# The output layer of a fused attention and feed-forward kernel: from two chunks at a time inside the gated streams to a stage of its own with seven products

## The chip, the cores and the metric

The kernel runs on one core of a Trainium2 chip. TensorE multiplies into PSUM; VectorE (DVE in the profile), ScalarE (ACT) and GpSimd (POOL) work on SBUF; SyncE (SP) issues the DMA transfers between SBUF and device memory. The metric is the device time of one execution in microseconds (us): the median of several runs. A profile comes from one further execution on the same core.

## The reference

Attention with a sigmoid, a feed-forward layer with a maximum of three products, and a gated feed-forward layer, one after the other:

```python
scores = scale * np.matmul(q, k.transpose(0, 1, 3, 2)) - np.log(S)     # q, k, v: 4 x 12 x 448 x 64
attn = np.matmul(1.0 / (1.0 + np.exp(-scores)), v)
x = np.ascontiguousarray(attn.transpose(0, 2, 1, 3)).reshape(B * S, H * D)       # 1792 x 768
h = np.maximum(np.maximum(x @ w1, x @ w2), x @ w3)                     # 768 x 768 each
x = h @ w_out                                                          # 768 x 768
g = x @ w_gate                                                         # 768 x 1536
silu = g * (1.0 / (1.0 + np.exp(-g)))
val = x @ w_val                                                        # 768 x 1536
return silu * val @ w_out2                                             # 1536 x 768; 1792 x 768 comes out
```

The change is about the last product, `silu * val @ w_out2`, and about how the products before it are summed. The weights come as 64-bit floats and are turned into 32-bit ones on the chip.

## The kernel before

Every matrix product is done with split operands: each 32-bit factor is a high part (a cast by ACT or DVE, L351) and a low part (the subtraction of the high part from the factor, on DVE or POOL, L354), and three of the four products of parts are added (`PRODUCTS`). So one product over 128 contraction rows is three matmul instructions, all of them from line L922.

The 1792 rows are worked in two parts: s=0 holds rows 0 to 767, s=1 rows 768 to 1791. A part is two blocks of n columns, n=384 for s=0 and n=512 for s=1. After attention come the first layer, the second layer, then `gated(1)` and `gated(0)`.

Four of the layers' products go through `stream` (L1051): a 768-wide factor is cut in halves both ways, and instead of eight block products seven products of sums of halves are made (A11·B11, S2·T2, A12·B21, S3·T3, A22·T4, S1·T1, S4·B22), nine matmuls each. Each product gets a PSUM bank of its own (`m` and `av` in turn), and DVE adds the bank to a running sum in SBUF (`plus`, L1078). The left factors of a stream (tiles `w`, a ring of five) come from DRAM in `gated(0)`: `gated(1)` stored them split (`ds_S`, `ds_A`), and `seven` loads them (L572) into the tiles (A11, A12), (S2, S3), (A22), (S1, S4). The right factors (tiles `T00` to `T26`) stay for all twelve streams of a part; for s=0 `recall` loads the rows kept in DRAM and makes them, with one instruction per 384 columns.

`gated(s)` runs six times over: a gate stream (whose four results go through Silu on ACT), a value stream (whose results are multiplied with those, L1148, and split into tiles `g`), and, one round late, `last(i)`: with the 256 rows of w_out2 that belong to i (tile `wr`, from `rows_pair`), each of the part's 128-row chunks (8 for s=1, 6 for s=0) gets two outputs of 384 columns, six matmuls each. The first round copies the two banks (tile `mm`) into an SBUF tile `o`; the next ones add to it (L1206, 768 wide); the final round adds 384 columns at a time (L1216) and sends them to `out` (L1223). The final `last` of `gated(1)` stands between the streams of `gated(1)` and those of `gated(0)`, and while it runs, `recall` is worked on DVE, ACT and POOL.

What sets the order: every step is a task with costs per engine and a due time, and a planner (`Plan.order`) lists them; each engine then works its list strictly in order, and waits at an instruction whose inputs are not there. The products keep program order on TensorE. SP too issues its DMAs in the listed order, each one when its tile is free.

## Time and profile before

| | |
|---|---|
| median of three runs | 975.11 us (974.92 to 975.33) |
| span of the profiled execution | 976.3 us |
| TensorE matmul busy | 961.4 us, 98% of the span, 5099 instruction records |
| VectorE busy | 646.9 us, 66% |
| ScalarE busy | 429.0 us, 44% |
| GpSimd busy | 147.2 us, 15% |
| DMA | 214 GB/s on the mean |
| `gated(1)` | about 498 to 766 us |
| `gated(0)` | about 766 to 976 us |

The profiled execution has no time other than its span, from the first to the last instruction; the span is 1.2 us over the median. Sums are made against the span, and 1.2 us is taken off at the end. "Busy" is a share of the whole span; which engine ends a wait differs from stage to stage, so the views of a stretch count for more than these shares. TensorE instructions overlap: the pitch from one group's start to the next one's start is what a group costs, and it is shorter than the busy time shown for it. The same holds for DVE.

### The profile page before, as it was taken

The numbers are of one execution on the slowest core, as the hardware profiler recorded it, in microseconds if no ns is written. First come the engines' busy times: TensorE is split into PE (matmuls) and PEld (weight loads), VectorE is DVE, ScalarE is ACT, GpSimd is POOL, SyncE is SP. The second block draws the span as 40 slices with busy tenths as digits, with TensorE's granted clock in tenths as the row PEclk, the third lists the DMA queues.
The fourth block names the chain that finished last, engine by engine and source line by source line (L and its number), as shares of the span: only waits on it lengthen the run. The fifth ranks groups of instructions, "written<-read, shape, count | busy, mean of one in ns | idle before, by whom it ended". The sixth has DMA issues, their size and how long they took to land.

```text
span 976.3 us, 13569 instructions
## 1 busy us (share of the span) xinstructions
PE 961.4 (98%) x5099; PEld 814.7 (83%) x5099; DVE 646.9 (66%) x971; ACT 429.0 (44%) x603; POOL 147.2 (15%) x117
## 2 busy tenths in 40 slices
PE   9989999999999999999999999999999999999998
PEld 4435677767999888888878989888898999999998
DVE  5565667676777888964588396958587743455545
ACT  5666576686666555513355461615253322111110
POOL 0100000000110132210012031425334300000000
PEclk9999999999999999999999999999999999999999
DMA  6677899997998755433357474847588865557532
GB/s 123 119 142 176 241 241 273 243 274 247 313 318 302 230 189 178 140 127 138 113 192 271 168 288 155 298 162 276 198 306 304 299 234 195 193 194 254 187 139 100
DMA packets 179297, 208.51 MB, mean 214 GB/s; under 512 B 98080, under 2 KB 154656, under 8 KB 179232
## 3 DMA queue, kind: packets, MB, share of 16 engines
q1 hardware_dynamic: 177376, 207.42, 66.6%
q8 instruction: 40, 0.66, 0.3%
q10 hardware_dynamic: 1856, 0.23, 0.2%
q14 instruction: 25, 0.20, 0.1%
HBM read 132.91 MB, written 74.71 MB: 213 GB/s over the span
## 4 chain that ended last, share of the span: by engine, by line
PE 81%; DMA 8%; DVE 4%; SPq 4%; issue 1%; ACT 1%; DVEq 0%; ACTq 0%
PE m L922 32%; PE av L922 25%; PE mm L922 18%; SPq L708 3%; PE av L805 3%; PE ps L776 2%; DMA wraw<-in_moe_w_out_dram 2%; DMA rk<-in_k_dram 1%; DMA dp<-c 1%; DMA rq<-in_q_dram 1%; DMA wraw<-in_moe_w_gate_dram 1%; DMA rv<-in_v_dram 1%; DMA wraw<-in_moe_w_val_dram 1%; DVE kT L746 0%; PE ps L769 0%
## 5 line engine op out<-in xcount | busy, mean ns | idle before, releaser
L922 PE MATMUL av<-T,w 128*128 128x512 f32 (+1 forms) x1044 | 235.8, 369 | 0.7 <-DVE T L354 0.7
L922 PE MATMUL m<-T,w 128*128 128x512 f32 (+1 forms) x1035 | 233.1, 369 | 0.0
L922 PEld LDWEIGHTS av<-T,w 128*128 128x128 f32 x1044 | 191.0, 188 | 26.7 <-DVE T L354 1.1
L922 PEld LDWEIGHTS m<-T,w 128*128 128x128 f32 x1035 | 189.5, 188 | 25.7
L922 PE MATMUL mm<-wr,g 128*128 128x384 f32 x840 | 147.7, 334 | 0.1
L922 PEld LDWEIGHTS mm<-wr,g 128*128 128x128 f32 x840 | 145.9, 188 | 0.9 <-DVE o L1206 0.4
L922 PEld LDWEIGHTS m<-x,w 128*128 128x128 f32 x648 | 112.4, 189 | 12.6 <-issue 8.1
L922 PE MATMUL m<-x,w 128*128 128x384 f32 x648 | 120.0, 340 | 0.0
L1078 DVE TENSOR_TENSOR u<-m,u 128x512 f32<-128x512 f32 (+1 forms) x75 | 48.1, 645 | 75.1 <-PE m L922 74.7
L789 ACT ACTIVATE a<-ps,bias 128x896 f32<-128x896 f32 x84 | 80.7, 1003 | 30.2 <-PE ps L776 25.8
L1206 DVE TENSOR_TENSOR o<-mm,o 128x768 f32<-128x768 f32 x56 | 53.4, 955 | 47.2 <-PE mm L922 47.2
L805 PE MATMUL av<-a,rv 128*64 128x448 f32 (+1 forms) x384 | 76.4, 562 | 2.0 <-DVE x L354 1.6
L776 PEld LDWEIGHTS ps<-qq,kk 64*128 64x128 f32 x432 | 45.4, 252 | 34.1 <-ACT a L789 23.9
L776 PE MATMUL ps<-qq,kk 64*128 64x448 f32 x432 | 61.0, 406 | 6.9 <-ACT a L789 6.7
L450 ACT ACTIVATE r<-wraw 128x768 int32<-128x768 uint32 x48 | 43.7, 911 | 50.9 <-DMA wraw<-in_moe_w_gate_dram 14.4
L354 POOL TENSOR_TENSOR g<-t,g 128x512 fp32r<-128x512 f32 (+1 forms) x21 | 28.3, 1348 | 249.7 <-ACT g L351 240.6
L471 DVE SCALAR_TENSOR_TENSOR c<-c,r 128x768 int32<-128x768 int32 x48 | 49.2, 1025 | 18.6 <-ACT r L463 17.9
L1078 DVE TENSOR_TENSOR u<-av,u 128x512 f32<-128x512 f32 (+1 forms) x72 | 45.9, 641 | 20.7 <-PE av L922 20.4
L351 ACT COPY u<-av 128x512 f32<-128x512 f32 (+1 forms) x17 | 9.3, 549 | 112.4 <-PE av L922 112.4
L805 PEld LDWEIGHTS av<-a,rv 128*64 128x64 f32 (+1 forms) x384 | 20.1, 136 | 39.0 <-issue 29.4
L463 ACT ACTIVATE r<-wraw 128x768 f16<-128x768 f32 x48 | 52.2, 1087 | 0.6
L351 ACT CAST g<-t 128x384 fp32r<-128x384 f32 (+1 forms) x43 | 23.9, 560 | 56.9 <-DVE t L1148 52.2
(109 smaller groups left out, 1104.8 us busy)
## 6 DMA issues: line engine op xcount, KB each, us to landing
ds_S<-w SPq DMA_DIRECT2D x24, 768.0 KB, 4.5
w<-ds_S SPq DMA_DIRECT2D x24, 768.0 KB, 5.1
dp<-c SPq DMA_DIRECT2D x42, 384.0 KB, 4.9
cc<-dp SPq DMA_DIRECT2D x21, 768.0 KB, 4.9
wraw<-in_moe_w_dram SPq DMA_DIRECT2D x18, 768.0 KB, 5.9
wraw<-in_moe_w_gate_dram SPq DMA_DIRECT2D x12, 768.0 KB, 5.8
wraw<-in_moe_w_val_dram SPq DMA_DIRECT2D x12, 768.0 KB, 5.1
ds_A<-w SPq DMA_DIRECT2D x12, 768.0 KB, 5.4
```

Source lines behind the costliest of these rows:

```text
L351: (eng.copy if eng is nc.scalar else eng.tensor_copy)(o, i)
L354: eng.tensor_tensor(out=o, in0=a, in1=b, op=ALU.subtract)
L450: lambda e: e.activation(rb_at(), word(0).bitcast(U32), AF.Copy, scale=0.875 * 2.0 ** -29, bias=0.4999),
L463: lambda e: e.activation(rb_at().bitcast(F16).rearrange("p (c two) -> p c two", two=2)[:, :, 1], word(1).bitcast(F32), AF.Copy, scale=2.0 ...
L471: lambda e: e.scalar_tensor_tensor(c_at().bitcast(I32), c_at().bitcast(I32), 3, rb_at(), ALU.logical_shift_left, ALU.bitwise_or),
L708: eng.dma_start(out=r.t[D * j + 32 * e:D * j + 32 * e + 32], in_=src[b, h0 + j, :, 32 * e:32 * e + 32].rearrange("(c i) d -> i c d", i=32),)
L776: nc.tensor.matmul(psb.t[:, j, :S], kk.t[half_p[j], wh, cols], qq.t[half_p[j], xh], start=(i == 0), stop=(i == 2),)
L789: lambda e: e.activation(ab.t, psb.t[:, :, :S], AF.Sigmoid, bias=bias, scale=SCALE),
L805: nc.tensor.matmul(accs[g].t[half_p[j], :S], pairs[g][2].t[at, j, c], ab.t[at, j], start=first[g], stop=last[g],)
L922: nc.tensor.matmul(acc.at(n), l(), r(), start=(i == 0), stop=(i == len(terms) - 1))
L1078: lambda e: e.tensor_tensor(out=o.t[:, :n], in0=acc.at(n), in1=x.t[:, :n], op=ALU.add),
L1206: lambda e, o=o, b=banks[0].b: e.tensor_tensor(out=o.t, in0=b.t[:, :, :NO], in1=o.t, op=ALU.add),
```

## The change

`last` and `rows_pair` go. The products of gate and value are no longer split there: those of s=0 stay in SBUF (tile `G0`), those of s=1 go to DRAM (24 stores of 256 KB), and a new stage `output` at the very end multiplies them with w_out2, again as seven products of sums of halves: the contraction (1536) and the 768 output columns are cut in halves, and so are the rows, where one chunk takes 128 rows of block 0 and 128 of block 1 of the same part. There are seven chunks (three of s=0, four of s=1), seven products each, 18 matmuls of 128x384 a product: 882, where `last` had 1008. The weights w_out2 are turned into 32-bit numbers during streams 2 to 9 of `gated(0)` and four streams of `gated(1)` (`rows_ahead`; 768 KB in, 384 KB out to DRAM each), and loaded again for the new stage (tile `W`, four loads). Sums and splits of both factors are made in the stage, on DVE, ACT and POOL.

In `stream` the products are reordered, and two products that are added go to the same bank: A12·B21 onto A11·B11, S3·T3 and A22·T4 onto S2·T2, S4·B22 onto S1·T1. Before a product is added to a bank, the earlier sum in the bank must have been read. A22·T4 is done late, behind A11·B11 of the next stream. The left tiles are loaded in the order (A11, A12), (S2, S3), (S1, S4), (A22). `recall` makes its sums with instructions of 3x384 columns. The evictions of attention get a due time (`FREE`).

```diff
-    LEFT = (("A11", "A12"), ("S2", "S3"), ("A22",), ("S1", "S4"))
+    LEFT = (("A11", "A12"), ("S2", "S3"), ("S1", "S4"), ("A22",))
...
-    RIGHT = ("B11", "T2", "B21", "T3", "T4", "T1", "B22")
+    RIGHT = ("B11", "T2", "T1", "B21", "T3", "B22", "T4")
...
     def stream(s, left, facs, use, into=None, gated_=True):
...
-        p1 = mult("A11", "B11")
+        mult("A11", "B11", one, True, False)
+        catch_up()
+        u0, w0 = plain(one)
+        mult("S2", "T2", two_, True, False)
+        u1 = half.buf("u", [P, 512])
+        w1 = plus(u1, two_, u0, "u")
+        mult("S1", "T1", three, True, False)
+        v5, w5 = plain(three)
+        mult("A12", "B21", one, False, True, w0)
...
+            use(0, 0, one)
...
+        mult("S3", "T3", two_, False, False, w1)
+        w2 = done(1, 1, two_, v5)
+        mult("S4", "B22", three, False, True, w5)
+        done(0, 1, three, u1)
+
+        def rest_():
+            mult("A22", "T4", two_, False, True, w2)
+            done(1, 0, two_, u0)
+
+        behind.append(rest_)
...
+    OUTER = ("A11", "A12", "S2", "S3", "A22", "S1", "S4")
...
+        def evict(o, acc, x, key=None):
+            plan.add(
+                {"dve": t_dve(NO)},
+                lambda e: e.tensor_tensor(out=o.t[:, :NO], in0=acc.at(NO), in1=x.t[:, :NO], op=ALU.add),
...
+        fetch_g(0)
+        fetch_w(2)
+        fetch_g(1)
+        for q in (1, 3, 0):
+            fetch_w(q)
+        for q in (2, 3):
+            fetch_g(q)
+        for x, name in enumerate(OUTER):
             plan.kind = "w"
...
+            wf = weights(x)
+            for s, c in chunks:
+                k = s, c
+                plan.kind = "w"
+                if name == "A12":
+                    sums(A, k, 2, 2, 3, ALU.add, (), True)
+                if name == "S2":
+                    sums(A, k, 0, 2, 0, ALU.subtract, read[s, c, "A11"])
+                if name == "S3":
+                    sums(A, k, 0, 3, 0, ALU.subtract, read[s, c, "S2"] + s4[k])
+                wb, hl = factor(s, c, name)
+                if name == "S2":
+                    s4[k] = sums(A, k, 1, 1, 0, ALU.subtract, read[s, c, "A12"], True)
```

Three places show the order. In the lists L922 of before is L926 of after, L1078 is L1160, L354 is L358, and L1148 is L1272.

**A stream of `gated(0)`, TensorE.** In the names, T01 is the right factor of the first third of the contraction for the product with index 1, `w_...` is the left tile, `m`, `av` and `mm` are banks. Before, from A11·B11 on:

```order
L922 MATMUL m_8647<-T00_6954,w_8474 128x384 x3
L922 MATMUL m_8647<-T10_6975,w_8474 128x384 x3
L922 MATMUL m_8647<-T20_7232,w_8474 128x384 x3
L922 MATMUL av_8663<-T01_6980,w_8599 128x384 x3
L922 MATMUL av_8663<-T11_7173,w_8599 128x384 x3
L922 MATMUL av_8663<-T21_7267,w_8599 128x384 x3
L922 MATMUL m_8679<-T02_6992,w_8474 128x384 x3
L922 MATMUL m_8679<-T12_6996,w_8474 128x384 x3
L922 MATMUL m_8679<-T22_7241,w_8474 128x384 x3
L922 MATMUL av_8691<-T03_7034,w_8599 128x384 x3
```

Now, of the second stream of `gated(0)`:

```order
L926 MATMUL m_6361<-T00_6115,w_6258 128x384 x3
L926 MATMUL m_6361<-T10_6117,w_6258 128x384 x3
L926 MATMUL m_6361<-T20_6119,w_6258 128x384 x3
L926 MATMUL mm_6261<-T06_6301,w_6239 128x384 x3
L926 MATMUL mm_6261<-T16_6303,w_6239 128x384 x3
L926 MATMUL mm_6261<-T26_6306,w_6239 128x384 x3
L926 MATMUL mm_6389<-T01_6194,w_6318 128x384 x3
L926 MATMUL mm_6389<-T11_6207,w_6318 128x384 x3
L926 MATMUL mm_6389<-T21_6209,w_6318 128x384 x3
L926 MATMUL av_6404<-T02_6173,w_6371 128x384 x3
L926 MATMUL av_6404<-T12_6184,w_6371 128x384 x3
L926 MATMUL av_6404<-T22_6187,w_6371 128x384 x3
```

The tile (A11, A12), w_8474 before, was read by the first and the third product; now (w_6258) by the first and the fifth. A22·T4 of the stream before (w_6239) stands second.

**The passage from `gated(1)` to `gated(0)`, DVE.** Before, behind the streams of `gated(1)`, the final additions of `last` (`o`) stand among the sums (L670) and splits of the right factors T:

```order
L1078 TENSOR_TENSOR u_6969<-av_7040,u_6969 128x512
L1216 TENSOR_TENSOR o_5289<-m_7061,o_5289 128x384
L1216 TENSOR_TENSOR o_5289<-av_7070,o_5289 128x384
L354 TENSOR_TENSOR g_7079<-t_6777,g_7079 128x512
L1216 TENSOR_TENSOR o_5308<-m_7083,o_5308 128x384
L1216 TENSOR_TENSOR o_5308<-av_7094,o_5308 128x384
L670 TENSOR_TENSOR u_7113<-cc_6868,u_6973 128x384
```

Now the last results of `gated(1)` (128x512), the right factors, and the first result of `gated(0)` (u_6324):

```order
L358 TENSOR_TENSOR T25_6255<-cc_6124,T25_6255 128x384
L1077 TENSOR_TENSOR S2_5349<-S2_5349,cc_6017 128x1152
L1160 TENSOR_TENSOR u_6153<-av_6143,u_6153 128x512
L1160 TENSOR_TENSOR u_6113<-mm_6126,u_6113 128x512
L358 TENSOR_TENSOR T06_6301<-S2_5349,T06_6301 128x384
L358 TENSOR_TENSOR T16_6303<-S2_5349,T16_6303 128x384
L358 TENSOR_TENSOR T26_6306<-S2_5349,T26_6306 128x384
L1272 TENSOR_TENSOR t_6065<-m_6086,t_6065 128x512
L1272 TENSOR_TENSOR t_6100<-u_6153,t_6100 128x512
L1272 TENSOR_TENSOR t_6139<-u_6113,t_6139 128x512
L1160 TENSOR_TENSOR u_6324<-mm_6261,u_6271 128x384
```

`u_6324<-mm_6261` reads the first sum of S2·T2 in `gated(0)`; until that is done, S3·T3 can't be added to the same bank. It stands behind all the rows above it. Twelve more splits of T (128x384, from `T01_6194` to `T15_6252`) stand ahead of the first row shown, and ahead of those the eviction of S3·T3 of the last stream of `gated(1)`. Matmuls of the last layer no longer lie in between.

**The new stage, DVE, in its second product (A12).** Evictions are L1419, sums L1383, splits L358; `w` is the factor of a chunk, `W`, `wr` and `wq` are the weights:

```order
L1419 TENSOR_TENSOR t_7804<-av_7758,p_7609 128x384
L1419 TENSOR_TENSOR t_7811<-m_7785,p_7636 128x384
L1383 TENSOR_TENSOR W_7524<-W_7524 128x768
L358 TENSOR_TENSOR w_7718<-G1_7515,w_7718 128x768
L1383 TENSOR_TENSOR W_7524<-W_7524 128x768
L358 TENSOR_TENSOR w_7753<-G1_7519,w_7753 128x768
L358 TENSOR_TENSOR wr_7747<-W_7524,wr_7747 128x2x384
```

Before, DVE had in a block of `last` nothing but the additions:

```order
L1206 TENSOR_TENSOR o_7601<-mm_8458,o_7601 128x768
L1206 TENSOR_TENSOR o_7616<-mm_8476,o_7616 128x768
L1206 TENSOR_TENSOR o_7631<-mm_8490,o_7631 128x768
L1206 TENSOR_TENSOR o_7646<-mm_8504,o_7646 128x768
L1206 TENSOR_TENSOR o_7661<-mm_8518,o_7661 128x768
```

The low part of chunk 5's factor (`w_7718`) now stands behind the eviction of chunk 4's product (`m_7785`), while TensorE takes chunk 5 right behind chunk 4.

## Rows read from the trace of the kernel before

**Rows 1.** The page: span, and busy time, share and instructions of each engine.

```profile
span 976.3 us, 13569 instructions
PE 961.4 (98%) x5099; PEld 814.7 (83%) x5099; DVE 646.9 (66%) x971; ACT 429.0 (44%) x603; POOL 147.2 (15%) x117
```

**Rows 2.** Windows: stretch, length, busy of five engines, granted clock, DMA share, GB/s.

```profile
316.00:444.50 128.50, 128.50 (x568) 106.36 (x568) 108.35 (x152) 59.87 (x81) 31.58 (x27) 1.00 0.55 179
498.50:749.60 251.10, 251.04 (x1219) 221.70 (x1218) 185.54 (x241) 104.74 (x150) 74.05 (x53) 1.00 0.68 245
749.64:766.31 16.67, 16.67 (x98) 16.66 (x96) 13.06 (x21) 4.78 (x10) 14.28 (x13) 1.00 0.77 262
769.40:959.70 190.30, 190.30 (x1100) 190.30 (x1099) 90.95 (x152) 34.20 (x65) 6.11 (x6) 1.00 0.57 201
```

**Rows 3.** TensorE's timeline: start, length, instructions, idle time before and its releaser.

```profile
46.99 0.97 PE L805 MATMUL av<-a,rv 128*64 128x448 f32 x4 [1.56 <-DVE x L354]
...
123.58 2.37 PE L776 MATMUL ps<-qq,kk 64*128 64x448 f32 x12 [2.04 <-ACT a L789]
...
497.82 0.73 PE L922 MATMUL av<-T,w 128*128 128x512 f32 x2 [0.69 <-DVE T L354]
```

**Rows 4.** Windows behind the first two of those idle times (the clock stands third from the end).

```profile
47.00:50.00 3.00, 3.00 (x20) 1.23 (x22) 1.34 (x3) 0.97 (x2) 0.68 (x1) 1.00 0.69 106
...
123.50:125.00 1.50, 1.42 (x8) 1.13 (x10) 0.00 (x0) 1.50 (x3) 0.00 (x0) 0.85 0.91 107
125.00:127.00 2.00, 2.00 (x9) 1.45 (x6) 1.55 (x3) 2.00 (x3) 0.00 (x0) 0.50 0.92 212
127.00:130.00 3.00, 3.00 (x16) 2.92 (x15) 1.98 (x4) 2.45 (x4) 0.00 (x0) 0.84 0.92 268
```

**Rows 5.** TensorE's timeline in `gated(0)`: a block of `last`, then products of a stream.

```profile
799.07 12.64 PE L922 MATMUL mm<-wr,g 128*128 128x384 f32 x72
811.55 1.72 PE L922 MATMUL av<-T,w 128*128 128x384 f32 x9
813.11 1.72 PE L922 MATMUL m<-T,w 128*128 128x384 f32 x9
814.67 1.72 PE L922 MATMUL av<-T,w 128*128 128x384 f32 x9
816.23 1.72 PE L922 MATMUL m<-T,w 128*128 128x384 f32 x9
```

**Rows 6.** Groups by line and shape: count, busy us, mean ns, idle before and releaser.

```profile
L1206 DVE TENSOR_TENSOR o<-mm,o 128x768 f32<-128x768 f32 x56 | 53.4, 955 | 47.2 <-PE mm L922 47.2
...
L354 DVE TENSOR_TENSOR w<-S,w 128x768 fp32r<-128x768 f32 x36 | 35.9, 996 | 2.3 <-ACT w L351 2.3
...
L1078 DVE TENSOR_TENSOR u<-m,u 128x512 f32<-128x512 f32 x51 | 34.8, 686 | 37.6 <-PE m L922 37.3
...
L354 POOL TENSOR_TENSOR w<-S,w 128x768 fp32r<-128x768 f32 x6 | 11.9, 2016 | 0.0
```

**Rows 7.** DVE's timeline: instructions back to back, and one beside POOL at 754.50.

```profile
734.83 1.81 DVE L1206 TENSOR_TENSOR o<-mm,o 128x768 f32<-128x768 f32 x2
736.57 0.94 DVE L354 TENSOR_TENSOR wr<-S,wr 128x768 fp32r<-128x768 f32 x1
...
754.50 1.14 DVE L670 TENSOR_TENSOR u<-cc,u 128x384 f32<-128x384 f32 x1
...
766.31 0.55 DVE L354 TENSOR_TENSOR T<-cc,T 128x384 fp32r<-128x384 f32 x1
766.78 0.55 DVE L670 TENSOR_TENSOR u<-cc,u 128x384 f32<-128x384 f32 x1
```

**Rows 8.** SP's timeline in `gated(0)`: start of a DMA's issue, length, line, what.

```profile
816.42 0.32 SPq L572 DMA_DIRECT2D w<-ds_S x1
```

**Rows 9.** DMA issues of 812 to 834, at 819.5, and of 673.5 to 690: count, KB, us to landing.

```profile
w<-ds_S SPq DMA_DIRECT2D x4, 768.0 KB, 5.4
w<-ds_A SPq DMA_DIRECT2D x2, 768.0 KB, 5.5
...
w<-ds_S SPq DMA_DIRECT2D x1, 768.0 KB, 6.4
...
cc<-in_moe_w_out_dram SPq DMA_DIRECT2D x1, 768.0 KB, 7.8
ds_A<-w SPq DMA_DIRECT2D x1, 768.0 KB, 9.1
```

More of the change, by code (lines that the diff above doesn't have):

```diff
@@ L76 @@
 OUT = 8000.0
+FREE = 12000.0
 OUTO = 8000.0
@@ L933, in product @@
         terms, needs = [], []
-        for kk in range(len(src)):
+        for kk in order:
             get, bufs = src[kk](blk)
```

534 lines of the change are left out of this document (351 added, 183 removed).

## Prediction, on record before the changed kernel ran

> **What bounds the kernel now.** I read the page first: TensorE's matmuls are busy for 98% of the span, and no other engine for more than 66% [rows 1]. The reader is to see that the kernel can only become faster by fewer matmuls or by a higher clock; any work taken from another engine is worth nothing by itself. Next come the windows by stage [rows 2]: from the first layer on TensorE has no gap worth naming, and the granted clock is 1.00, the 2.4 GHz level. DVE is at 84% in the first layer of s=1 (108.35 of 128.50 us), at 74% in the streams of `gated(1)`, and at 48% in `gated(0)`. So in `gated(0)`, where much of the new work lies, other engines have room, and in `gated(1)` there is less. Then TensorE's timeline, for its idle times: the only one behind the first layer is 0.69 us [rows 3]. It shows what a wait costs beyond itself. Behind a wait of 2.04 us for ACT the clock was 0.85, 0.50 and 0.84 in the next 6.5 us [rows 3, 4]: 1.5 x 0.15 + 2 x 0.5 + 3 x 0.16 = 1.7 us lost at the 1.2 GHz level. Behind a wait of 1.56 us for DVE it stayed at 1.00 [rows 3, 4]. So I charge a wait near 2 us or longer 1.7 us more, and shorter ones nothing.
>
> **What is removed.** `last` issues 14 chunks x 2 halves x 6 rounds x 6 = 1008 matmuls of 128x384; the new stage 7 chunks x 7 products x 18 = 882. A block of 72 takes 811.55 - 799.07 = 12.48 us from its start to the next product's start [rows 5], 173.3 ns each. 126 fewer are 21.8 us. All of that lies on the path, since TensorE is full. The number of matmuls in the streams does not change, nor does the end (an eviction of 384 columns and a transfer of the same size behind the last product). DVE also loses 56 additions of 0.955 us [rows 6], which bring nothing, since TensorE did not wait for them.
>
> **What is added: the passage to `gated(0)`.** The final block of `last` in `gated(1)` is 16.67 us of matmuls, while DVE worked 13.06 us and POOL 14.28 us on, among other things, the right factors of s=0 [rows 2]. That cover is gone. Let E be the end of the last product of `gated(1)`. In the new order DVE first evicts S3·T3, which ends two products of 512 columns ahead of E, so at about E - 4.1 (2 x 9 x 173.3 ns x 512/384 = 4.16 us, an estimate from [rows 5], a little long, as not all of a matmul's time grows with its columns). Behind it, strictly in order, stand 16 splits of 384 columns, a sum of 1152, two evictions and three multiplications of 512, and only then the eviction that S3·T3 of the first stream waits for. By the pitch of back-to-back instructions, 0.47 us at 384 (766.78 - 766.31) and 0.87 at 768 (half of 736.57 - 734.83) [rows 7], the line between them gives 0.60 at 512 and 1.27 at 1152: 16 x 0.47 + 1.27 + 6 x 0.60 (the first eviction counted in) = 12.4 us. From E - 4.1 + 0.25 the awaited eviction begins at E + 8.6 and ends at E + 9.1. By whole durations, 0.55 and 0.686 [rows 6, 7], it ends near E + 11. TensorE reaches S3·T3 after four products, at 4 x 1.56 = 6.24 us [rows 5]. The stall is 2.9 to 4.8 us; I take 3.9, as ACT has to make the high parts first, and add 1.7 for the clock: **+5.6**. At best (no loss of clock) it is 2.9.
>
> **The new stage.** DVE's order forces one wait in the second product: evict chunk 4 (0.47), one sum of weights (0.87), the low part of chunk 5's factor (0.996 [rows 6]) stand between TensorE's end of chunk 4 and its start of chunk 5. That is 2.4 us with the 0.2 us until DVE sees the bank, near the row of 2.04, so 1.7 us of clock more: +4.1. In front of the first chunk of S3 stand one eviction, three sums, one low part of a factor, three low parts of weights and one more factor: 0.47 + 7 x 0.87 + 0.996 = 7.6 us at most against two products of 3.12 (18 x 173.3 ns), +0 to 1.3 us; I take 0.6. Between those DVE is about 94% busy, by counting its instructions in the order at these pitches. POOL makes 14 sums of 768, 2.0 us each [rows 6], beside it. A subtraction of DVE beside POOL took 1.14 us instead of 0.55 [rows 7]. If half of the 14 sums cost DVE 0.6 us each, that is 4 us, of which I let three quarters fall into what slack there is: +1.3. All together **+6.0**, with bounds of 2 (DVE gets ahead, no clock lost) and 14 (each of the 14 sums costs DVE 0.6 us, all of it waited for). The Trainium skill, GPSIMD Engine Reference, section Specifications, says that POOL shares its SBUF interfaces with VectorE and contends with DVE instructions that have two SBUF inputs. Nearly all sums and splits here are of that kind; by that rule each sum of POOL would slow them and the upper bound is the nearer one, while the trace has both kinds of row beside POOL.
>
> **Weights in `gated(0)`.** The ring of left tiles has five places, a stream takes four. Before, the shortest time from the release of a place to the need for what is loaded there was five products; in the new order it is four, for (S2, S3) and for (S1, S4): 6.24 us. SP issued 0.19 us after the tile was free (816.42 against 816.23) [rows 5, 8], so a load has 6.05 us. The loads of this stretch took 4.4 to 6.4 us, 5.4 in the median [rows 9]. The transfers become denser too: streams 2 to 9 each carry 768 KB of w_out2 in and 384 KB out beside their own weights, 3.9 MB in 10.9 us or about 360 GB/s by counting, where the stretch had 201 on the mean [rows 2]. I take 0.3 to 0.4 us late for each of 12 streams: **+4**. The ends are 0 (as in the trace, 5.4 us in the median) and 12 (1 us late each time).
>
> **The rest.** In the streams, each addition to a bank waits for the reading of the earlier sum; between them lie two products (3.1 or 4.1 us) or more, and an eviction takes 0.56 to 0.69 us, so it costs nothing as long as DVE's list isn't late. In the first layer of s=1 DVE goes from 84% to about 92% by the count of instructions. In `gated(1)` the DMA goes from 245 GB/s to some 340, since the same streams lie closer together. What cover is left there is the queue of prepared tiles. I take **+1** for both, from -1 (the wait of 0.69 us goes) to 8.
>
> **Sum.** 976.3 - 21.8 + 5.6 + 6.0 + 4 + 1 = 971.1 us of span. The profiled run is 1.2 us above the median of the runs: 969.9 us.
>
> A rule speaks against the clock's share in this sum. In the trace a wait for ACT's reading of PSUM was followed by 0.50 [rows 3, 4]. The Trainium skill, TensorE: Matmul & The Clock Gate, section "Loop structure matters more than you think", says that copying results out of PSUM behind dense matmuls doesn't break TensorE's warmth, and that long waits for DMA do. By it the two charges of 1.7 us would fall away and the sum would be 966.5; I go by the rows.
>
> **Rivals.**
> *Nothing is late.* DVE and ACT get ahead in the list, and loads land as before. For it: DVE has been at 48% in `gated(0)`. Against it: the two forced waits follow from the order alone. It gives 976.3 - 21.8 - 1.2 = 953.3, and 958 with the two waits at their shortest (2.9 and 2).
> *The gain is eaten by the new stage.* DVE becomes the bound in S2 and S3 because POOL slows it (the upper bound, 14): 971.1 + 8 - 1.2 = 977.9, and 973.9 with half of it.
> *Slower: the left tiles of `gated(0)` come late.* Loads at the end of dense stretches took 7.8 to 9.1 us [rows 9]. At 8 us a load is 8 - 6.05 = 1.95 us late, and a wait of that length costs 1.7 us of clock more: 3.65 us in each of the eight streams that carry w_out2, +29 in place of +4, so about 995 us. It decides from a landing of some 7.4 us on (8 x 1.4 = 11 us): below that the sum stays under 977. For it: four products in place of five, and denser transfers. Against it: none of the loads in the `gated(0)` rows reached 7 us.
> *The change doesn't do what it says.* The order lists 882 matmuls of the new stage and the same number in the streams; I give this nothing.
>
> **Chances.** A measurement of this kernel can tell about 0.2% from no change, so "same" is 973.2 to 977.1. The sum as it stands, 961 to 973: 0.57. Nothing late, 953 to 958: 0.10. Gain eaten, 973 to 978: 0.18. Late tiles, above 978: 0.15. The range of 8 in 10 reaches from 957 to 977.5. Faster 0.67, same 0.17, slower 0.16.
>
> **What would show it.** In the changed profile: matmuls of the last stage 49 x 3.12 = 153 us when full; a TensorE gap of 3 to 5 us in the first stream of `gated(0)`, released by DVE's eviction, and behind it a stretch at half clock; a gap near 2.4 us before chunk 5 of A12; small gaps released by DMA `w<-ds_S` or `w<-ds_A` in `gated(0)`; landings there of 6 to 7 us. It would be wrong if the landings are at 8 us, if TensorE is idle in the last stage for more than 10 us, or if gaps show in `gated(1)` or in the first layer, for which I charged next to nothing.

## The result, and the profile after

The changed kernel takes 983.62 us in the median of four runs (981.52 to 988.01), the kernel before 975.22 us (974.92 to 976.69): a ratio of 1.0087, with an interval of 1.006 to 1.0114. It is slower, and outside the range of the prediction (957 to 977.5). The profiled execution is the longest of the four, with a span of 986.2 us and a time of 988.01. In this and every later profile the time is about 1.8 us over the span. So the 1.2 us by which the prediction goes from the span to the median compares a span with times: the profiled execution of before stood for about 978.1 us (an estimate from its span), 3 us above its median, and that of after is 4.4 us above its own. The ledger below is one of spans; its 9.9 us stand for 8.4 us between the medians.

The first two lines of the page (span; busy time, share and instructions of each engine) answer to [rows 1]:

```profile
span 986.2 us, 13350 instructions
PE 948.9 (96%) x4973; PEld 797.7 (81%) x4973; DVE 664.9 (67%) x1000; ACT 437.6 (44%) x606; POOL 97.1 (10%) x67
```

The reader sees that TensorE has 126 instructions fewer and 12.5 us less of busy time, and that it is no longer full. Windows by stage (stretch, length, busy time of PE, PEld, DVE, ACT and POOL, clock, DMA share, GB/s) answer to [rows 2]. They are, in turn, the first layer of s=1, the second layer, the streams of `gated(1)`, those of `gated(0)`, and the new stage:

```profile
317.97:455.93 137.96, 131.61 (x569) 108.07 (x568) 114.71 (x172) 68.19 (x95) 16.02 (x12) 0.98 0.58 196
455.93:504.89 48.96, 48.96 (x218) 40.54 (x216) 29.77 (x48) 20.44 (x34) 0.00 (x0) 1.00 0.43 155
504.89:676.25 171.36, 171.36 (x758) 141.89 (x756) 134.06 (x201) 60.33 (x97) 16.96 (x13) 1.00 0.86 302
676.25:824.74 148.49, 137.75 (x757) 133.07 (x756) 69.63 (x120) 43.77 (x72) 1.74 (x2) 0.98 0.83 286
824.74:982.56 157.82, 155.00 (x883) 154.21 (x882) 120.25 (x143) 52.51 (x68) 34.94 (x16) 0.99 0.28 104
```

Length minus PE's busy time is TensorE's idle time: none in `gated(1)` (and that at 302 GB/s), 6.35 us in the first layer, 10.7 in `gated(0)`, 2.8 in the new stage. The waits of TensorE (who waits, for whom: us in total, times, longest) name the releasers:

```profile
PE mm L926 <- ACT T L355: 6.4, 1, 6.4
PE ps L778 <- ACT a L791: 6.1, 3, 5.3
PE av L926 <- DMA w<-ds_S: 5.6, 7, 1.6
PE mm L926 <- DVE u L1160: 3.8, 1, 3.8
PE av L807 <- ACT xf L355: 3.8, 1, 3.8
PE av L926 <- DVE w L358: 2.5, 1, 2.5
...
PE mm L926 <- DMA w<-ds_S: 1.2, 3, 0.6
```

The lines at L778 and L807 are attention's. The kernel before had waits of its own there, and one of 0.69 us behind attention [rows 3].

**The ledger of the difference.** The starts of the stages are read from TensorE's timeline. A full stage takes its number of matmuls times the pitch: 756 x 173.3 ns = 131.04 us in `gated(0)`, 882 x 173.3 ns = 152.9 in the new stage.

| part | before | after | what the sum had | measured |
|---|---|---|---|---|
| 1008 matmuls become 882 | 174.7 us | 152.9 us | -21.8 | -21.8 |
| passage to `gated(0)` | | wait 3.81, clock 2.7 | +5.6 | +6.55 |
| new stage, over 152.9 | | 157.8 | +6.0 | +4.9 |
| left tiles, the rest over 131.04 | | 148.49 | +4 | +10.9 |
| the rest: first layer of s=1 | 128.56 | 137.96 | in +1 | +9.4 |
| the rest: attention up to the first layer of s=1 | 315.82 | 317.97 | in +1 | +2.15 |
| the rest: second layer, `gated(1)`, end | | | in +1 | -2.2 |
| span | 976.3 | 986.2 | 971.1 | 986.2 |

Of the four added terms, the passage and the new stage came out about as worked out; the one for left tiles was too small by 6.9 us and "the rest" by 8.35.

**The first layer.** TensorE's timeline at its start (start, length, instructions, idle before and releaser):

```profile
317.97 2.24 PE L926 MATMUL m<-T,w 128*128 128x512 f32 x9
320.05 1.52 PE L926 MATMUL mm<-T,w 128*128 128x512 f32 x6
327.93 1.95 PE L926 MATMUL mm<-T,w 128*128 128x512 f32 x3 [6.35 <-ACT T L355]
```

The second product, S2·T2, has done two thirds of its contraction (six matmuls) and waits for the right factor of the last third. That factor is made from attention's output, which comes back from DRAM. SP's timeline has the load (`cc<-dx`), of after and, in the second fence, of before:

```profile
318.09 0.58 SPq L890 DMA_DIRECT2D cc<-dx  x1
```

```profile
307.42 0.32 SPq L886 DMA_DIRECT2D cc<-dx  x1
```

It is issued 10.7 us later. It also took longer to land, among other transfers (KB, us to landing; of after, and of before):

```profile
cc<-dx SPq DMA_DIRECT2D x1, 512.0 KB, 7.8
```

```profile
cc<-dx SPq DMA_DIRECT2D x1, 512.0 KB, 3.7
```

What the issue waited for stands in DVE's timeline of after: the two instructions that read a tile `cc` of the ring of two, for the left tile of A22, are done at 318.01:

```profile
317.06 0.35 DVE L355 CAST w<-cc 128x384 fp32r<-128x384 f32 x1
317.45 0.56 DVE L358 TENSOR_TENSOR w<-cc,w 128x384 fp32r<-128x384 f32 x1
```

A22 is now the last of the four left tiles, and until it has been split it keeps the source tile that the load needs. Behind these waits the clock (third from the end) was, for the 6.35 us, then for the 3.81 us at the passage, then for two waits for DMA in `gated(0)`:

```profile
328.00:330.00 2.00, 2.00 (x4) 1.37 (x5) 2.00 (x4) 1.92 (x4) 0.00 (x0) 0.50 0.96 244
330.00:332.00 2.00, 2.00 (x6) 1.52 (x6) 2.00 (x4) 0.00 (x0) 0.00 (x0) 0.50 0.62 200
332.00:340.00 8.00, 8.00 (x34) 6.50 (x33) 6.58 (x11) 3.63 (x6) 0.29 (x1) 0.91 0.68 244
686.00:690.00 4.00, 3.51 (x11) 3.52 (x12) 2.81 (x5) 3.37 (x5) 0.00 (x0) 0.50 1.05 356
690.00:694.00 4.00, 4.00 (x20) 4.00 (x19) 1.80 (x3) 1.13 (x3) 0.00 (x0) 0.77 0.96 320
720.00:724.00 4.00, 3.05 (x17) 3.05 (x18) 0.99 (x2) 1.12 (x2) 0.00 (x0) 1.00 1.01 411
768.00:771.00 3.00, 2.04 (x11) 2.04 (x12) 0.00 (x0) 0.10 (x1) 0.00 (x0) 1.00 1.00 304
```

**The passage.** DVE's timeline behind the end of `gated(1)` (676.25) shows the list that the prediction counted, with its last rows here, and TensorE's first product behind the wait:

```profile
684.08 0.68 DVE L1272 TENSOR_TENSOR t<-m,t 128x512 f32<-128x512 f32 x1
684.68 1.27 DVE L1272 TENSOR_TENSOR t<-u,t 128x512 f32<-128x512 f32 x2
685.89 0.54 DVE L1160 TENSOR_TENSOR u<-mm,u 128x384 f32<-128x384 f32 x1
```

```profile
686.49 3.25 PE L926 MATMUL mm<-T,w 128*128 128x384 f32 x9 [3.81 <-DVE u L1160]
```

**Left tiles in `gated(0)`.** A part of one stream in TensorE's timeline: A22·T4 of the stream before, then S2·T2 and S1·T1; a product alone has a pitch of 1.56 us [rows 5]:

```profile
763.34 1.72 PE L926 MATMUL mm<-T,w 128*128 128x384 f32 x9
765.51 1.86 PE L926 MATMUL mm<-T,w 128*128 128x384 f32 x9 [0.45 <-DMA w<-ds_S]
768.96 1.85 PE L926 MATMUL av<-T,w 128*128 128x384 f32 x9 [1.59 <-DMA w<-ds_S]
```

These are the two tiles that the prediction named: (S2, S3) waits in three streams, (S1, S4) in seven. The loads (count, KB, median us to landing), of after and, in the second fence, of before:

```profile
w<-ds_S SPq DMA_DIRECT2D x20, 768.0 KB, 6.5
```

```profile
w<-ds_S SPq DMA_DIRECT2D x20, 768.0 KB, 4.8
```

**The new stage.** TensorE at chunk 5 of A12, and DVE ahead of it: an eviction, a sum of weights, the awaited low part, as predicted:

```profile
865.02 4.79 PE L926 MATMUL av<-wq,w 128*128 128x384 f32 x17 [2.51 <-DVE w L358]
```

```profile
862.38 0.56 DVE L1419 TENSOR_TENSOR t<-m,p 128x384 f32<-128x384 f32 x1 [2.56 <-PE m L926]
862.85 1.25 DVE L1383 TENSOR_TENSOR W<-W 128x768 f32<-128x768 f32 x1
864.02 0.94 DVE L358 TENSOR_TENSOR w<-G,w 128x768 fp32r<-128x768 f32 x1
```

### The profile page after: what moved, and what is told of

Its sections match the earlier page's. It is cut to its first block, busy times and chain, and to the rows that moved or that the text cites. A ratio compares the mean times of both kernels' runs of the same rounds, so it can differ in the third digit from the quotient of the medians.

```text
span 986.2 us, 13350 instructions
## 1 busy us (share of the span) xinstructions
PE 948.9 (96%) x4973; PEld 797.7 (81%) x4973; DVE 664.9 (67%) x1000; ACT 437.6 (44%) x606; POOL 97.1 (10%) x67
## 4 chain that ended last, share of the span: by engine, by line
PE 73%; DMA 15%; DVE 5%; SPq 3%; ACT 3%; issue 1%; DVEq 0%; ACTq 0%
PE m L926 25%; PE av L926 20%; PE mm L926 18%; DMA w<-ds_S 6%; PE av L807 5%; PE ps L778 4%; SPq L710 2%; DMA wraw<-in_moe_w_out_dram 2%; DMA wraw<-in_moe_w_val_dram 2%; DMA dp<-c 1%; DVE T L358 1%; DMA rk<-in_k_dram 1%; DMA cc<-dx 1%; ACT r L468 1%; PE ps L771 1%
## 5 line engine op out<-in xcount | busy, mean ns | idle before, releaser
L926 PE MATMUL mm<-T,w 128*128 128x512 f32 (+1 forms) x891 | 200.0, 373 | 11.4 <-ACT T L355 6.4
L926 PEld LDWEIGHTS mm<-T,w 128*128 128x128 f32 x891 | 164.2, 189 | 36.1 <-ACT T L355 6.8
L926 PE MATMUL av<-T,w 128*128 128x512 f32 (+1 forms) x594 | 137.8, 377 | 5.7 <-DMA w<-ds_S 5.6
L926 PE MATMUL m<-T,w 128*128 128x512 f32 (+1 forms) x594 | 133.9, 369 | 0.0
L926 PEld LDWEIGHTS av<-T,w 128*128 128x128 f32 x594 | 110.8, 192 | 23.8 <-DMA w<-ds_S 8.5
L926 PEld LDWEIGHTS m<-T,w 128*128 128x128 f32 x594 | 108.9, 188 | 14.9
L926 PEld LDWEIGHTS m<-x,w 128*128 128x128 f32 x648 | 111.7, 188 | 10.2 <-issue 4.8
L926 PE MATMUL m<-x,w 128*128 128x384 f32 x648 | 118.1, 338 | 1.4 <-DVE t L355 1.1
L1160 DVE TENSOR_TENSOR u<-mm,u 128x512 f32<-128x512 f32 (+1 forms) x93 | 59.0, 634 | 43.8 <-PE mm L926 43.1
L807 PE MATMUL av<-a,rv 128*64 128x448 f32 (+1 forms) x384 | 76.3, 567 | 4.5 <-ACT xf L355 3.8
L778 PEld LDWEIGHTS ps<-qq,kk 64*128 64x128 f32 x432 | 45.3, 251 | 32.3 <-ACT a L791 21.9
L778 PE MATMUL ps<-qq,kk 64*128 64x448 f32 x432 | 59.7, 403 | 6.3 <-ACT a L791 6.1
L807 PEld LDWEIGHTS av<-a,rv 128*64 128x64 f32 (+1 forms) x384 | 20.3, 137 | 44.7 <-issue 34.8
L358 DVE TENSOR_TENSOR w<-G,w 128x768 fp32r<-128x768 f32 x49 | 50.3, 1035 | 3.5 <-ACT w L355 3.5
L926 PE MATMUL av<-wr,w 128*128 128x384 f32 x288 | 52.5, 334 | 0.0
L926 PEld LDWEIGHTS av<-wr,w 128*128 128x128 f32 x288 | 50.1, 188 | 0.0
```

Of the source, the lines that this page charges most:

```text
L358: eng.tensor_tensor(out=o, in0=a, in1=b, op=ALU.subtract)
L778: nc.tensor.matmul(psb.t[:, j, :S], kk.t[half_p[j], wh, cols], qq.t[half_p[j], xh], start=(i == 0), stop=(i == 2),)
L807: nc.tensor.matmul(accs[g].t[half_p[j], :S], pairs[g][2].t[at, j, c], ab.t[at, j], start=first[g], stop=last[g],)
L926: nc.tensor.matmul(acc.at(n), l(), r(), start=first and i == 0, stop=last and i == len(terms) - 1, skip_group_check=not (first and last),)
L1160: lambda e: e.tensor_tensor(out=o.t[:, :n], in0=acc.at(n), in1=x.t[:, :n], op=ALU.add),
```

## The experiments

The theory, formed from these rows: the stage is worth what it says, and the loss comes from the streams' new order, through three places (first layer, passage, left tiles). The rivals: the new stage itself is at fault, or the added transfers are, or attention's due times. All ratios are to the kernel before in the same comparison, with the 95% interval. The ledger of every profile, in us (start of the first layer of s=1, then the length of each stage, each up to the end of its last product by the pitch):

| run | start | first layer | second | `gated(1)` | `gated(0)` | last stage | median us, ratio |
|---|---|---|---|---|---|---|---|
| full stages | | 128.5 | 48.96 | 171.36 | 131.04 | 152.9 | |
| after | 317.97 | 137.96 | 48.96 | 171.36 | 148.49 | 157.8 | 983.62, 1.0087 |
| after_again | 318.93 | 137.04 | 48.96 | 171.36 | 144.61 | 157.6 | 983.15, 1.0078 |
| a22_early | 319.10 | 133.66 | 49.80 | 171.36 | 146.52 | 157.6 | 979.58, 1.0044 |
| half_loads | 318.05 | 137.09 | 48.96 | 171.36 | 138.01 | 158.0 | 975.82, 1.0002 |
| pool_free | 316.55 | 136.35 | 48.96 | 171.36 | 148.74 | 159.4 | 985.63, 1.0103 |
| less_traffic | 315.84 | 136.53 | 48.96 | 173.35 | 142.66 | 156.1 | 979.25, one run |
| no_free | 318.25 | 135.42 | 48.96 | 171.36 | 145.98 | 156.7 | 982.08, one run |
| pool_splits | 318.49 | 136.44 | 48.96 | 171.36 | 146.43 | 159.4 | 986.52, one run |
| all_three | 316.59 | 134.52 | 48.96 | 171.36 | 138.79 | 157.8 | 969.61, 0.9944 |
| gates_first | 317.11 | 134.13 | 48.96 | 171.36 | 133.89 | 156.5 | 967.62, one run |
| less_pool | 314.14 | 137.68 | 48.96 | 171.36 | 135.44 | 152.9 | 963.88, 0.9887 |
| stage_alone | 318.00 | 130.65 | 49.20 | 177.78 | 132.98 | 157.8 | 966.58, 0.9904 |
| old_streams_tuned | 316.68 | 129.84 | 49.21 | 171.36 | 134.79 | 152.9 | 958.44, 0.9816 |

**after_again**, the changed kernel without an edit.

> The changed kernel once more, unaltered, as a yardstick on the same chip. Its four runs so far lay between 981.5 and 988.0 us, wider than those of the kernel before. If the spread comes from transfers that land at different times (theory), its waits for DMA and for the third load of x should differ between profiles while the waits set by the order alone (3.8 us before S3 of the first stream of gated(0), 2.5 us in the A12 product of the last stage) should stay within 0.3 us. The rival, that the spread is the chip's, would show in before too.

983.15 us, 1.0078 [1.0063, 1.0094]: the loss is repeatable, and so are the waits (6.0 us for ACT in the first layer, 3.8 at the passage, 2.3 in the new stage). Those for left tiles vary: 3.6 us in seven places here, 6.8 in ten in after. The medians don't show that the changed kernel spreads more than the other: in this comparison it took 981.37 to 984.0 us, and the kernel before 973.54 to 977.84.

**a22_early**, the left tile of A22 made third for the first set alone.

```diff
+        if first:
+            tile_of(LEFT[3], [cc], lambda: a(3))
         tile_of(LEFT[2], [s1, s4], lambda: sb.t[:, 2:4].rearrange("p a c -> p (a c)"))
-        tile_of(LEFT[3], [cc], lambda: a(3))
+        if not first:
+            tile_of(LEFT[3], [cc], lambda: a(3))
```

> In the very first set of left tiles (first stream of the first layer of s=1) A22 is made third again, as before the change, so that its source tile cc comes free earlier for the third pair of x. Theory: TensorE's wait of 6.35 us in that stream comes from the load of x (cc<-dx) that was issued only when the A22 split had released cc; with the tile free earlier the wait falls below 1 us and the clock loss behind it (2.8 us) goes: 8 to 9 us less in the profile, about 975 to 978. Rival: the load is late because SP's queue ahead of it and DMA landings of 7 to 8 us hold it; then the issue moves by less than 2 us and at least 3 us of wait stay.

979.58 us, 1.0044 [1.003, 1.0058]. That is short of the 975 to 978 us of the theory. The load is issued at 312.37, and the wait for ACT is gone. A smaller one takes its place, this time for an eviction; TensorE and DVE:

```profile
329.92 2.99 PE L929 MATMUL mm<-T,w 128*128 128x512 f32 x9 [2.12 <-DVE u L1163]
```

```profile
327.77 1.03 DVE L594 TENSOR_TENSOR S<-cc 128x384 f32<-128x384 f32 x2 [2.36 <-DMA cc<-dp]
...
329.18 0.69 DVE L1163 TENSOR_TENSOR u<-mm,u 128x512 f32<-128x512 f32 x1
```

The eviction stands in DVE's list behind sums that wait for a weight's DMA, and the next product is added to the same bank. So the cause of the 6.35 us holds, but only 3.4 to 4.3 us of the layer's 9.4 came back with it (133.66 us, against 137.04 in after_again and 137.96 in after). The waits that are left in the layer, 2.12 and 0.41 us, are both for the eviction of a bank that is added to.

**half_loads**, each left tile of `gated(0)` loaded by two transfers, one per factor.

```diff
+                def load(_, wb=wb, d=d, n=n):
+                    for at in [slice(h, h + HC) for h in range(0, n, HC)]:
+                        nc.sync.dma_start(out=wb.t.bitcast(F32)[:, :, at], in_=d.t[:, :, at])
...
```

> Each left tile of gated(0) is loaded by two DMAs, one for each factor in it, so the factor that is needed first no longer waits for the other. Same tiles, same order, same bytes. Theory: the waits for w<-ds_S (6.8 us in ten places, 11 us with what each costs beside it) come from a load of 768 KB needing longer than the four products it has; the first half of 384 KB lands sooner by 1 to 2 us, and at least 8 of the 11 us go: about 972 to 978. Rival: DMA engines are full in this stretch (284 GB/s, share 0.83), the first half is held up by other transfers all the same, and at most a third of it goes.

975.82 us, 1.0002 [0.9986, 1.0019]. TensorE waits for a left tile only once more, for 0.22 us; `gated(0)` is 10.5 us shorter than in after, 6.6 shorter than in after_again, and 7.0 us over its full length, of which the passage is 6.5. The loads of (S2, S3) and (S1, S4):

```profile
w<-ds_S SPq DMA_DIRECT2D x40, 384.0 KB, 5.7
```

Whether the earlier landing alone does it, or also that a half can be loaded as soon as its old content has been read, this run doesn't tell apart.

**less_traffic**, the eight of the twelve conversions of w_out2 that lie in `gated(0)` left out; the four of `gated(1)` are stored three times each in their place.

```diff
-                if 2 * i + j in ROWS[s]:
+                if s and 2 * i + j in ROWS[s]:
...
```

> In gated(0) the eight conversions of w_out2 are left out, with their loads (768 KB) and stores (384 KB) and their work on ACT and DVE; the four of gated(1) are stored three times each, so the last stage multiplies with repeated weights. Left tiles are loaded in one DMA each, as in the changed kernel. Theory: the late left tiles come from two things at once, four products of lead and 1.2 MB more per stream; without the traffic loads land in 5.0 to 5.5 us and the waits for w<-ds_S fall from 3.4 to 6.8 us to below 1 us. Rival: the lead alone does it; then the loads in the streams that never had the extra traffic are late as well, and at least half of the waits stay.

One run, 979.25 us. Loads of 768 KB land in 5.2 us, and the waits for left tiles are 3.1 us in seven places, none over 0.91 (after: 6.8 in ten, up to 1.59; after_again: 3.6 in seven). `gated(0)` takes 142.66 us, against 148.49 and 144.61. The theory, less than 1 us of waits, missed. Both hold a part: without this traffic the shorter lead still leaves waits, and the traffic adds 2 to 6 us; its size isn't fixed better by two profiles that differ by 3.9 us.

**pool_free**, the planner no longer keeps DVE's sums apart from POOL's in the new stage.

```diff
-            if e == "pool" or e == "dve" and t.port:
+            if t.port:
...
-                reads=[xb, yb], writes=[ob], wait=wait, port=True,
+                reads=[xb, yb], writes=[ob], wait=wait, port=not pool,
```

> The planner no longer treats the sums that POOL makes in the last stage as blocking DVE, so DVE's list in that stage changes and nothing ahead of it. Theory: the 2.5 us wait in the A12 product is set by DVE's order alone; it and the 1.7 us of clock behind it go, 4 us less: about 978 to 983. Rival: POOL's sums slow DVE's two-input instructions and DVE is the bound there in any order; then waits of 2 us or more stay in the stage, at the same or another chunk.

985.63 us, 1.0103 [1.0083, 1.0122]. The wait of A12 is gone, and three evictions are late instead, by 2.3, 1.3 and 0.5 us:

```profile
PE av L926 <- DVE t L1419: 2.3, 1, 2.3
```

The stage gets 1.6 to 1.8 us longer, not 4 shorter. That fits the rival: with POOL's sums beside it DVE has no room for this work, whichever instruction comes first. The run less_pool tries it from the other side.

**pool_splits**, some splits and a sum at the passage given to POOL, which the planner no longer keeps apart from DVE's work.

```diff
-            if e == "pool" or e == "dve" and t.port:
+            if t.port:
...
-                {"dve": t_dve(HD * n), "pool": t_pool(HD * n)},
+                {"pool": t_pool(HD * n)} if o == "B21" else {"dve": t_dve(HD * n), "pool": t_pool(HD * n)},
...
-                    tb, [part], at, n, lambda tb=tb: tb.t[:, 0, :n], lambda tb=tb: tb.t[:, 1, :n], None,
+                    tb, [part], at, n, lambda tb=tb: tb.t[:, 0, :n], lambda tb=tb: tb.t[:, 1, :n], None, name in ("B22", "T4"),
...
```

> At the passage to gated(0) the splits of the right factors for S4 and A22 and the sum for T4 are made by POOL instead of DVE: 6 splits of 384 and a sum of 1152, about 4 us of DVE's list ahead of the eviction that S3 of the first stream waits for. Theory: that list is the cause of the 3.8 us wait and of the 2.6 us of clock behind it; both go, about 6 us in the profile. Rival: ACT, which makes the high parts, or POOL itself sets it; then the wait moves to the splits on POOL (S4 or A22 of the first streams) and at least 2 us stay.

One run, 986.52 us. The theory missed: the wait at the passage falls only to 2.62 us, with 0.50 of clock behind it. DVE's two multiplications beside POOL took 2.80 us, where after has 1.27 for the same:

```profile
678.51 2.80 DVE L1272 TENSOR_TENSOR t<-u,t 128x512 f32<-128x512 f32 x2
```

**no_free**, attention's due times of before.

```diff
-FREE = 12000.0
+FREE = math.inf
```

> The due time that the change gave to attention's evictions is taken away; DVE and ACT get attention's old order of priorities. Theory: the first stream of s=1 starts 2 to 3 us later than before the change (318.0 to 318.9 against 315.8, in profiles) because of this reordering, whose two waits of TensorE, for ACT's scores and for the copy of the tail columns (xf), are 5 and 4 to 5 us; without it that stream starts near 316 and the xf wait is below 1 us. Rival: the ring sizes (tiles that moved) do it, and the start stays at 318 or later.

One run, 982.08 us; the first layer of s=1 begins at 318.25, not near 316. So taking the due times away doesn't bring attention's 2.15 us back.

**all_three**, the edits of a22_early, half_loads and pool_splits together.

> half_loads, a22_early and pool_splits together. Theory: the costs sit in different places and add up: 983 less 8 (half loads), 4 (A22 earlier), 6 (passage) gives 965 us, 10 below the kernel before. Rival: a wait removed is given back at the next place, as with a22_early, where 3.6 of 9 us were won; then it is 968 to 974.

969.61 us, 0.9944 [0.9925, 0.9964]: the changed kernel is faster than before once these waits are small. It lies in the rival's range (968 to 974), not at the theory's 965: a wait of 2.63 us stayed at the passage, one of 1.93 came in the first layer, and 1.8 us in three places for left tiles, halved loads or not.

**gates_first**, a22_early and half_loads, and the multiplications of the last stream of `gated(1)` early in DVE's list.

```diff
-                    reads=[src.b, t], writes=[t if s else G.quarter[q]], port=True, due=due_p + 4000.0,
+                    reads=[src.b, t], writes=[t if s else G.quarter[q]], port=True,
+                    due=due_p - 80000.0 if s and i == KG // 2 - 1 else due_p + 4000.0,
```

> On top of half_loads and a22_early, the last three multiplications of gated(1) (gate times value) get an early due time, so that they stand ahead of the splits of the right factors; the eviction that S3 of the first stream of gated(0) waits for stood behind them because it takes one of the four u tiles that they read. POOL's part is not enlarged. Theory: the wait of 3.8 us at the passage is DVE's list ahead of that eviction (u tiles included); it falls below 1 us, with no POOL contention as in pool_splits, where 2.6 stayed: about 969 to 972. Rival: the same DVE work has to be done before the first stream is over; the wait returns later in the first two streams, at A22 or S4, and 2 us or more stay in sum.

One run, 967.62 us: `gated(0)` is down to 133.89 us and has no wait at the passage. That settles what the wait of 3.81 us was: the order of DVE's list.

**less_pool**, gates_first with the seven sums for S4 left to either engine instead of to POOL.

```diff
-                    s4[k] = sums(A, k, 1, 1, 0, ALU.subtract, read[s, c, "A12"], True)
+                    s4[k] = sums(A, k, 1, 1, 0, ALU.subtract, read[s, c, "A12"])
```

> gates_first, and in the last stage the seven sums for S4 may go to DVE, so POOL has seven sums of 768 fewer to make beside it. Theory: in the last stage DVE is slowed by POOL (a sum of 768 took 2.4 to 2.6 us instead of 0.95 while POOL ran); with half of POOL's sums gone DVE does the work sooner in spite of seven more sums, the wait of 2.5 us in A12 goes and no new one above 1 us comes: 4 us less than gates_first, 963 to 968. Rival: DVE is at its limit there and seven more sums (6 us) make evictions late, as in pool_free; waits of 2 us or more stay in the stage.

963.88 us, 0.9887 [0.9866, 0.9908]. The last stage is full: 152.9 us. The order of the first layer came out otherwise, with waits of 2.95 (ACT), 1.45 and 1.14 us (DVE) there.

**stage_alone**, the new stage with the streams in their order of before: one bank a product, sums in SBUF, A22 third.

```diff
-    LEFT = (("A11", "A12"), ("S2", "S3"), ("S1", "S4"), ("A22",))
+    LEFT = (("A11", "A12"), ("S2", "S3"), ("A22",), ("S1", "S4"))
...
-    RIGHT = ("B11", "T2", "T1", "B21", "T3", "B22", "T4")
+    RIGHT = ("B11", "T2", "B21", "T3", "T4", "T1", "B22")
...
-        mult("S3", "T3", two_, False, False, w1)
-        w2 = done(1, 1, two_, v5)
...
+        plus(u[2], mult("S3", "T3"), u[1], key)
+        plus(u[3], mult("A22", "T4"), u[2], "t" if into else key)
```

> The new last stage with the streams as they were before the change: seven products in the old order, each in a bank of its own, left tiles in the old order with A22 third; partial sums in SBUF share the four u tiles (before there were four more, v). Theory: what was lost in the first layer (9.4 us) and most of what was lost on left tiles (10.9 us) comes from the streams' new order, not from the stage; without it the gain of 21.8 us less some 5 us in the stage and up to 6 us at the passage remains: 962 to 970. Rival: the loss in gated(0) comes from streams that lie closer together and from more transfers; then waits for w<-ds_S of 5 us or more stay, and with fewer tiles for partial sums it is at 975 or above.

966.58 us, 0.9904 [0.988, 0.9927]. This takes some 17 us off the changed kernel. The first layer is at 130.65 us and `gated(0)` at 132.98. There TensorE waits for left tiles only twice, for 0.29 and 0.18 us, although these land about as late as in after (6.5 us):

```profile
w<-ds_S SPq DMA_DIRECT2D x18, 768.0 KB, 6.4
```

So with the old lead of five products the same landing isn't late, while with four products it was, even at 5.2 us (less_traffic). One wait stands in the last stream of `gated(1)`, and with its clock makes that stage 6.4 us longer:

```profile
671.62 4.21 PE L926 MATMUL av<-T,w 128*128 128x512 f32 x9 [4.29 <-DVE u L1149]
```

**old_streams_tuned**, stage_alone with three edits.

```diff
-        u += [half.buf("u", [P, 512]) for _ in range(1 if into else 2)]
+        u += [two.buf("v", [P, 512]) if gated_ and j == 0 else half.buf("u", [P, 512]) for j in range(1 if into else 2)]
...
-                due=due_p - OUT,
+                due=due_p - OUT - RUSH * sum(hurry),
...
-                    s4[k] = sums(A, k, 1, 1, 0, ALU.subtract, read[s, c, "A12"], True)
+                    s4[k] = sums(A, k, 1, 1, 0, ALU.subtract, read[s, c, "A12"])
```

> The kernel stage_alone (new last stage, the streams in their order of before) with three edits: one temporary of the accumulated sums in a small buffer of its own, so that the evictions of a gated stream wait less for each other; the evictions of the last stream of gated(1) ahead of what else VectorE has in its list; S4's sums of the last stage left to either of VectorE and GpSimd, as in less_pool. Theory (the loss of the changed kernel came from the streams' new order, and what was left in stage_alone were the 4.29 us wait in the last stream of gated(1), with its clock charge about 6.4 us, and 4.9 us in the last stage, which less_pool brought to none): 966.6 - 6.4 - 4.9 = about 955 us, 953 to 960. Rival (the evictions that are put first hold back the left tiles' sums of gated(0), which then come late, or the first product again waits for VectorE): one wait goes and another of 3 to 6 us comes in gated(0)'s first two streams; 961 to 966 us.

958.44 us, 0.9816 [0.9795, 0.9838]: the best of all, 1.8% faster than before. `gated(1)` lost its 6.4 us and the last stage its 4.9, as expected. Of the rival there is one wait, in the first stream of `gated(0)`; with the clock behind it (0.50 from 678 to 680) it is all of the 3.75 us by which that stage is over its full length:

```profile
676.86 2.65 PE L927 MATMUL av<-T,w 128*128 128x384 f32 x9 [1.78 <-DVE u L1152]
```

## Why the prediction was wrong

- **What bounds the kernel, and the matmuls: right.** `gated(1)` and, where no wait is left, the last stage run at exactly the count of matmuls times the pitch. The 21.8 us came in full.
- **The passage: right.** The awaited eviction ran from 9.6 to 10.2 us behind the end of `gated(1)` (9.1 to 11 was said for its end), and TensorE waited 3.81 us (3.9 said). The clock cost about 2.7 us instead of 1.7. gates_first shows the mechanism.
- **The new stage: right, 4.9 us for 6.0.** The wait in A12 was 2.51 us (2.4 said; the parts as given add up to 2.54), the one ahead of S3 0.31 (0.6). The share of POOL's sums, a quarter of some 4 us, is about 1.0 and not 1.3; the two slips cancel. DVE beside POOL was slower than in the row that the term rested on: two of its sums of 768 columns took 2.60 us each (0.95 alone), but little of that reached TensorE. pool_free gained nothing from another order, and in less_pool the loss goes with seven of POOL's sums.
- **Left tiles of `gated(0)`: the mechanism right, the term mis-sized, 10.9 us for 4** (by the same reckoning 7.0 in after_again, 144.61 - 131.04 - 6.55). The term took each load 0.3 to 0.4 us late, which with a lead of 6.05 us is a landing of some 6.4 us, and 6.5 came, as the DMA share went from 0.57 [rows 2] to 0.83. What it had wrong is what that costs: the waits come unevenly (0.2 to 1.6 us, in ten places, 6.8 us in sum), and the streams lost 10.9 us. Of the 4.1 us between the two some 0.3 for each wait is accounted for in the last section, the rest isn't. That the lead of four products decides, more than the traffic, is shown by two runs: 0.5 us of waits with the old lead at about the same landing (stage_alone), 3.1 us with the new lead at a landing of 5.2 (less_traffic). The upper bound, 12, was the nearer end.
- **"The rest": the step that failed, 9.35 us for 1.** The term weighed the first layer by DVE's share (84%, then some 92%), and DVE was in fact busy for 83% of the longer stretch. The 9.4 us there are one wait of 6.35 us and 3.05 of clock. The wait came from the moment at which a transfer can start, of which a busy share shows nothing: a left tile that moved to the end of its set kept a source buffer, so that a load of attention's output was issued 10.7 us later. Its landing, 7.8 us instead of 3.7, adds some 4.1 us of the 6.35 (an estimate, the difference of the two). The diff's first line, the new order of `LEFT`, was read only for `gated(0)`, where the tiles come from DRAM; in the first layer they are made on the chip from the ring of `cc`. A second loss shows when this one is taken away (a22_early): an addition to a bank waits 2.12 us for an eviction that is late in DVE's list. The term put that at nothing "as long as DVE's list isn't late". The prediction's closing sentence named gaps in the first layer as what would make it wrong.
- **Attention: open.** The kernels with the new stage reach the first layer of s=1 at 314 to 319 us, before was at 315.82. after, after_again, pool_free, pool_splits, half_loads and less_traffic, for which DVE's instructions up to there come in the same order, spread over 3.1 us by themselves (315.84 to 318.93). So the 2.15 us of one profile are within what one and the same list varies by, and a loss here isn't shown. These kernels share a wait of 3.3 to 4.8 us for the high part `xf`, which before didn't have, and after lacks the wait of 2.04 us [rows 3]. no_free keeps a late start without the due times; what else set that order wasn't tried.
- **The clock: the rows held, the rule as it was applied didn't.** The passage charged the clock behind a wait for an eviction, and it was at 0.50 there. The Trainium skill's sentence (TensorE: Matmul & The Clock Gate, "Loop structure matters more than you think") that copying out of PSUM doesn't break the warmth stands for a loop whose next matmuls follow immediately. The prediction applied it to a wait for such a copy, and by that the forecast would have been lower still. Nor did it matter here what is waited for: the longest wait for DMA, 2.08 us in pool_free, was followed by 0.50 too.
- **The rivals.** The time lay where "late left tiles" had put it, above 978, but only partly for that reason: landings stayed at 6.5 us, where it asked for 7.4. half_loads, which takes nearly all of those waits away, is level with before (975.82 us); a22_early alone leaves a loss of 0.44%. With both and pool_splits' edit (all_three) the kernel is 0.56% faster than before, and with the streams' old form, from which both causes are absent, 0.96% (stage_alone). So that this rival's range was hit is in part luck. Of the two rows on which it rested, the 9.1 us are those of a store (`ds_A<-w`), not of a load.

## What to carry to other kernels

When a diff changes the order in which tiles are made, follow for each place where that order is used which source buffer a later tile still holds, and which transfer waits for that buffer; a busy share shows nothing of it. When a change adds transfers, take the landing times from the densest stretch of the trace, not from the one that is to be filled, and compare the latest of them, not the median, with the new lead. An eviction that must be done before the next product may be added to the same bank turns the whole of DVE's list ahead of it into TensorE's wait. A bank of its own for each product gives such a list more time, but not without end: stage_alone still had a wait of 4.29 us for an eviction.

## What the runs showed of the hardware

- **The clock's price hardly follows the length of the wait.** Beyond the waits and the full length, a wait of 1.78 us cost 2.0 (`gated(0)` of old_streams_tuned), 2.51 and 0.31 together 2.1 (the new stage), 3.81 some 2.7 (the passage); in the first layer 4.50 cost 3.5 (less_traffic), 4.88 cost 2.0 (no_free) and 6.35 cost 3.05 (131.61 of busy time where before had 128.56). Behind the 3.81 and the 6.35 us the clock was at 0.50, the 1.2 GHz level, for about 4 us, then rose.
- **Short waits mostly left the clock alone, whatever they were for.** Behind waits for DMA of up to 1.61 us (a22_early) it stayed at 1.00, also where a stream had two of them; behind 1.78 us for DVE (old_streams_tuned) and 2.08 for DMA (pool_free) it fell to 0.50. Two waits close together, 0.27 us for ACT and 1.40 for DVE (first layer of gates_first), were followed by 0.50 as well.

```profile
766.47 2.24 PE L926 MATMUL av<-T,w 128*128 128x384 f32 x9 [2.08 <-DMA w<-ds_S]
```

- **A short wait costs more than its idle time shows.** In the rows at 763.34 to 768.96 the pitches are 2.17 us (0.45 idle in it) and 3.45 (1.59 idle) where a product takes 1.56: 0.16 and 0.30 us more than the idle time. 0.16 of each is the drawing: a product is shown 1.72 us long at a pitch of 1.56. The rest is that the first product behind a wait is shown 1.85 or 1.86 us long.
- **DVE beside POOL.** In the new stage, while POOL works (2.17 to 2.42 us a sum), DVE's sums with both inputs in SBUF are slowed by up to a factor of 2.7, and an eviction from PSUM isn't. DVE's timeline, then POOL's:

```profile
842.66 0.95 DVE L1383 TENSOR_TENSOR G<-G 128x768 f32<-128x768 f32 x1
...
844.13 2.60 DVE L1383 TENSOR_TENSOR G<-G 128x768 f32<-128x768 f32 x1
...
857.90 0.54 DVE L1419 TENSOR_TENSOR t<-av,p 128x384 f32<-128x384 f32 x1
```

```profile
843.75 2.17 POOL L1383 TENSOR_TENSOR G<-G 128x768 f32<-128x768 f32 x1 [10.90 <-DVE G L1383]
846.88 2.42 POOL L1383 TENSOR_TENSOR G<-G 128x768 f32<-128x768 f32 x1 [0.96 <-DVE G L1383]
852.79 10.49 POOL L1383 TENSOR_TENSOR G<-G 128x768 f32<-128x768 f32 x5 [3.49 <-DMA G<-dg]
```

That agrees with the Trainium skill (GPSIMD Engine Reference, Specifications), which names DVE instructions with two SBUF inputs as those that contend; the size is this trace's.
- **Two transfers of 384 KB instead of one of 768** landed in 5.7 us instead of 6.5 in about the same stretch. Waits for them were 0.2 us in sum in half_loads, but 1.8 in all_three, 0.7 in gates_first and 2.0 in less_pool, which have the same halves.
